# Attention and a routed mixture of experts in one kernel: gathers of tokens written ahead of gathers of weights, the token split written one group earlier, and the last tile's two blocks written to separate tiles

## The chip, the cores and the metric

The kernel runs on one core of one Trainium2 chip. The metric is device time in microseconds (us) of one execution. Three executions of the kernel before gave 2227.25, 2227.33 and 2228.41 us, median 2227.33. A further execution was recorded by the profiler; all rows quoted below come from it.

## The reference

```
def _attn_ref(u, v, z):            # u, v: 8 x 2496 x 256, z: 8 x 2496 x 64, f32
    scores = (1.0 / S) * np.matmul(z, z.transpose(0, 2, 1))
    attn = np.maximum(scores, 0.0) ** 2
    return u * np.matmul(attn, v)

def _moe_ref(x, w_gate, w1, w2):   # x: 19968 x 256, 8 experts, F = 1024
    logits = x @ w_gate
    expert_idx = np.argmax(logits, axis=1)
    ...
    gate_w = probs[np.arange(N), expert_idx]
    for e in range(E):
        mask = expert_idx == e
        xe = x[mask]
        h = np.maximum(xe @ w1[e], 0.0)
        out[mask] = gate_w[mask, None] * (h @ w2[e])
    return out
```

The attention output, reshaped to 19968 tokens of 256 values, is the input of the experts. Each token goes to one expert and is scaled by that expert's softmax probability.

## The kernel before

**Two stages.** For about the first 1310 us the attention of the 8 batches runs, and its rows are written to DRAM (`xrows`) together with the gate and the chosen expert. While it runs, lists are built that sort the tokens by expert. Then come 47 expert tiles (i = 0 to 46), and these are what the change touches. A tile holds k = 4, 3 or 2 blocks of 128 tokens of one expert. The k = 2 tiles (6, 10, 15, 17, 20, 25, 27, 31, 35, 37, 41, 46) and the k = 3 tiles (14, 24, 34, 45) are strewn among the k = 4 tiles. F = 1024 is walked in 8 slices of 128: a k = 4 or 3 tile takes one slice a step (G = 8 groups), a k = 2 tile two slices a step (G = 4 groups).

**What one tile needs.** Values are kept as a rounded part and a remainder, so that each product is three matmuls. The steps, with their lines in the profile of before:

- `load_e(i)`, L696: POOL gathers the tile's entries (token numbers and gates) into `ent`, a ring of 6. A slot comes free when the tile six earlier has had its output scattered.
- `load_x(i)`, L712: POOL gathers the tile's tokens into `rows` (ring of 3), one indirect DMA for each block. It reads the token numbers in `ent`.
- `load_w(w, h)`, L681: POOL gathers half of an expert's weights (1 MB) into a slot `s`. A slot comes free when the pieces cut from it have been read.
- `split_piece(q)`: ScalarE (ACT) L731 and L733 cast a piece of the weights to a rounded copy, VectorE (DVE) L732 and L734 subtract. The results are tiles `t` or `s`.
- `turn_x(i)`, L742: DVE transposes 32 x 32 cells of `rows` into a buffer `th`; then SP sends it to DRAM and back (L745, L747, `far`) into a second buffer `th`. The ring `th` has 3 buffers.
- `split_x(i)`: ACT L757 casts the turned tokens, DVE L758 subtracts. It frees one buffer `th`.
- `up(gi)`: PE L775 (tokens times first weights, into `ph`), ACT L779 relu, DVE L780 remainder. It is written two groups ahead of its use.
- `down(gi)`: PE L796 and L798 add into `y` (two PSUM tiles for a tile of 3 or 4 blocks, one for 2).
- `finish(i)`: ACT L806 and DVE L807 scale `y` by the gate into an output tile, POOL L809 scatters it, one indirect DMA for each block. Reading `y` frees it for the next tile.

**What sets the order.** `tiles()` writes these steps in program order, as the code printed below shows; a scheduler then orders the instructions of each engine by dependences and modelled times. What is wrapped in `pinned` goes right behind the last instructions written; `split_x` is, `turn_x` is not. On the chip each engine takes its instructions in the scheduled order. At a tile's first group (g = 0) the weights of later pieces are written first, then `load_x(i + 3)` and `load_e(i + 4)`; `turn_x(i + 2)` is written at g = G/2, and `split_x(i + 1)` at g = G - 3: group 5 of 8, or 1 of 4.

**The end.** After tile 46 (k = 2) each engine loads a count (`values_load`, L992) and branches on it: for these inputs the further tiles are skipped (L1014, L1016).

Of the kernel before, what the change touches and what calls it, by code (L numbers as in the profile page):

```python
# [8 lines left out]
F32 = mybir.dt.float32  # L9
# [10 lines left out]
P = 128  # L20
KQ = 64
G, R = 4, 32
D = 256
E = 8
F = 1024
QC = 512
# [22 lines left out]
def fused_kernel(ctx: ExitStack, tc: tile.TileContext, zt, ut, v, wg, wcat, out):  # L49
    nc = tc.nc  # L50
    B, _, SP = zt.shape
# [3 lines left out]
    NTOK = B * S  # L55
# [8 lines left out]
    BS, SS = BIG // P, SMALL // P  # L64
    ND, NB, N3, NS = split_sizes(NTOK - NA * 2 * BIG)
# [3 lines left out]
    ps2 = ctx.enter_context(tc.tile_pool(name="ps2", bufs=2, space=PSUM))  # L69
    ps1 = ctx.enter_context(tc.tile_pool(name="ps1", bufs=3, space=PSUM))  # L70
    psm = ctx.enter_context(tc.tile_pool(name="psm", bufs=1, space=PSUM))
# [9 lines left out]
    def ring_f():  # L81
        return sb.tile([P, 2, QC], F32, name="tf", tag="tf", bufs=3)
# [280 lines left out]
    def pinned(work):  # L363

        last = {}
        for i in nc.cur_bb.bb.instructions[-400:]:
            last[i.engine] = i
        with ExitStack() as behind:
            for i in last.values():
                behind.enter_context(tc.issue_after(i))  # L370
            work()
# [284 lines left out]
    MAIN = 12  # L656
# [6 lines left out]
    NM = len(order)  # L663
# [3 lines left out]
    own = [t not in seconds[which] for which, t, _ in order]  # L667
    wof = [sum(own[:i + 1]) - 1 for i in range(NT)]
# [8 lines left out]
    def load_w(w, h):  # L677
        which, t, _ = order[first_of[w]]
        wr = slot(free[0])
        free.append(free.pop(0))  # L680
        nc.gpsimd.indirect_dma_start(out=wr, out_offset=None, in_=wcat,  # L681
                                     in_offset=bass.IndirectOffsetOnAxis(ap=lists[which]["widx"][:, h, t:t + 1], axis=0))
        weights[w, h] = wr
# [100 lines left out]
    def down(gi, hh, hl):  # L784
        i, g = groups[gi]
        k = blocks[i]
        n = k * P
        w2 = pieces[piece_of[gi]][1]
        if g == 0:
            yts[i] = [ps2.tile([P, 2, QC], F32, name=f"y{s}", tag="ps2") for s in range(-(-k // 2))]  # L790
        for s in range(k):
            for c in range(fs_of[i]):
                f = g * fs_of[i] + c
                y = yts[i][s // 2][:, s % 2, :]
                cs = slice(c * n + s * P, c * n + (s + 1) * P)
                nc.tensor.matmul(y, lhsT=hh[:, cs], rhs=w2[:, f % 2].rearrange("p i d -> p (i d)"),  # L796
                                 start=f == 0, stop=False)
                nc.tensor.matmul(y[:, 0:D], lhsT=hl[:, cs], rhs=w2[:, f % 2, 0, :], start=False, stop=f == NF - 1)  # L798

    def finish(i):  # L800
        which, t, k = order[i]
        yo = ring_f().rearrange("p a (b d) -> p (a b) d", d=D)
        for s in range(k):
            y = yts[i][s // 2][:, s % 2, :]
            gate = ents[i][:, s, 0:1]
            nc.scalar.mul(yo[:, s, :], y[:, D:2 * D], gate)  # L806
            nc.vector.scalar_tensor_tensor(yo[:, s, :], y[:, 0:D], gate, yo[:, s, :], op0=ALU.mult, op1=ALU.add)  # L807
        for s in range(k):
            d = nc.gpsimd.indirect_dma_start(  # L809
                out=out, out_offset=token(i, s),  # L810
                in_=yo[:, s, :], in_offset=None, bounds_check=NTOK - 1, oob_is_err=False)
            for o in outs:
                tc.declare_no_dep(d.ins, o.ins, reason="rows are distinct")
            outs.append(d)
        del ents[i]
# [145 lines left out]
    def tiles(lo, hi, n_pieces):  # L961

        mine = [gi for gi, (i, _) in enumerate(groups) if lo <= i < hi]
        for gi in mine:
            i, g = groups[gi]
            G = NF // fs_of[i]
            if bg:
                pinned(bg.pop(0))
            if g == 0:
                for w, h in ((wof[i] + 1, 1), (wof[i] + 2, 0)):  # L970
                    if own[i] and w <= wof[hi - 1]:
                        load_w(w, h)
                if i + 3 < hi:
                    load_x(i + 3)
                if i + 4 < hi:
                    load_e(i + 4)
            ahead = min(gi + LU, mine[-1])
            while n_pieces < min(piece_of[ahead] + LP + 1, NPC * (wof[hi - 1] + 1)):
                split_piece(n_pieces)
                n_pieces += 1  # L980
            if i + 2 < hi and g == G // 2:
                turn_x(i + 2)
            if i + 1 < hi and g == G - 3:
                pinned(lambda: split_x(i + 1))
            if gi + LU <= mine[-1]:
                hs[gi + LU] = up(gi + LU)
            down(gi, *hs.pop(gi))
            if g == G - 1:
                finish(i)

    tiles(0, NM, n_pieces)
    needed = nc.values_load(lists["F"]["ns"], min_val=0, max_val=NS)  # L992

    def more(lo, hi):

# [15 lines left out]
        hs.update({gi: up(gi) for gi in range(first, first + LU)})  # L1011
        tiles(lo, hi, NPC * w + LP + 1)

    with tc.If(needed > MAIN):  # L1014
        more(NM, NM + 3)
        with tc.If(needed > MAIN + 3):  # L1016
            more(NM + 3, NT)


# [30 lines left out]
```

## Time and profile before

| | |
|---|---|
| median of 3 executions | 2227.33 us (2227.25 to 2228.41) |
| the profiled execution | 2225.69 us |
| its span | 2223.9 us |
| mean granted clock of PE | 0.997 |
| PE busy | 2197.9 us (99%) |
| DVE busy | 1678.0 us (75%) |
| ACT busy | 1313.2 us (59%) |
| POOL busy | 697.4 us (31%) |
| DMA, mean over the span | 194 GB/s |

The profiled execution is 1.64 us under the median, and its span 1.79 us under its own time; what lies around the span is outside the profile. A row of the timeline, as quoted further down, has the start in us, the duration, the engine, the line, the operation, output<-inputs, and in brackets how long the engine stood idle before it and whose end it waited for. Rows with x2 are two instructions in a row.

### The profile page before, as it was taken

The numbers are of one execution on the slowest core, as the hardware profiler recorded it, in microseconds if no ns is written. First come the engines' busy times: TensorE is split into PE (matmuls) and PEld (weight loads), VectorE is DVE, ScalarE is ACT, GpSimd is POOL, SyncE is SP. The second block draws the span as 40 slices with busy tenths as digits, with TensorE's granted clock in tenths as the row PEclk, the third lists the DMA queues.
The fourth block names the chain that finished last, engine by engine and source line by source line (L and its number), as shares of the span: only waits on it lengthen the run. The fifth ranks groups of instructions, "written<-read, shape, count | busy, mean of one in ns | idle before, by whom it ended". The sixth has DMA issues, their size and how long they took to land.

```text
span 2223.9 us, 32938 instructions
## 1 busy us (share of the span) xinstructions
PE 2197.9 (99%) x11664; PEld 1854.1 (83%) x11664; DVE 1678.0 (75%) x2782; ACT 1313.2 (59%) x1808; POOL 697.4 (31%) x720
## 2 busy tenths in 40 slices
PE   9999999999999999999999999999999999999997
PEld 6888888888888888888888888888888888888886
DVE  9888888888888888888888787566565575666653
ACT  8658657657667667667577544445454454554543
POOL 3010220220220220310222644455455455555521
PEclk9999999999999999999999999999999999999998
DMA  7966867858868758768857884565465465656530
GB/s 248 260 174 219 240 154 234 233 153 246 223 166 242 222 151 256 209 165 255 214 148 219 221 265 146 160 193 167 148 215 184 151 209 175 199 164 218 170 106 23
DMA packets 271884, 430.64 MB, mean 194 GB/s; under 512 B 109099, under 2 KB 167152, under 8 KB 252256
## 3 DMA queue, kind: packets, MB, share of 16 engines
q1 hardware_dynamic: 239200, 308.92, 48.8%
q0 software_dynamic: 32512, 119.55, 16.9%
q8 instruction: 93, 1.52, 0.3%
q14 instruction: 79, 0.65, 0.1%
HBM read 262.68 MB, written 166.20 MB: 193 GB/s over the span
## 4 chain that ended last, share of the span: by engine, by line
PE 90%; DVE 3%; DMA 2%; issue 2%; ACT 1%; POOL 1%; SPq 0%; POOLq 0%; DVEq 0%; ACTq 0%
PE ph L775 17%; PE acc L359 15%; PE acc L356 15%; PE acc L358 15%; PE y L796 12%; PE y L798 6%; PE ps_s L321 4%; PE ps_s L322 4%; PE pt L411 1%; DMA scr<-s 1%; DMA rows<-xrows,ent 1%; POOL out_dram L809 0%; POOL rows L712 0%; DVE tlo L335 0%; ACT tf L329 0%
## 5 line engine op out<-in xcount | busy, mean ns | idle before, releaser
L480 POOL DMA_INDIRECT lst<-gw,posi x160 | 201.3, 1258 | 872.0 <-DVE posi L477 535.6
L359 PE MATMUL acc<-thi,t 128*128 128x512 f32 (+1 forms) x1200 | 461.3, 386 | 0.0
L356 PE MATMUL acc<-thi,t 128*128 128x512 f32 (+1 forms) x1200 | 450.5, 386 | 0.6 <-DVE thi L333 0.6
L358 PE MATMUL acc<-tlo,t 128*128 128x512 f32 (+1 forms) x1144 | 443.0, 387 | 1.1 <-DVE tlo L335 1.1
L780 DVE SCALAR_TENSOR_TENSOR t<-ph,t 128x512 fp32r<-128x512 f32 (+1 forms) x328 | 220.0, 672 | 227.5 <-ACT t L779 223.6
L779 ACT ACTIVATE t<-ph 128x512 fp32r<-128x512 f32 (+1 forms) x328 | 192.8, 588 | 334.8 <-PE ph L775 304.2
L796 PE MATMUL y<-t,t 128*128 128x512 f32 x1062 | 378.6, 396 | 1.4 <-DVE tf L807 1.4
L775 PE MATMUL ph<-thi,t 128*128 128x512 f32 (+2 forms) x1248 | 375.6, 360 | 0.5 <-DVE t L780 0.3
L329 ACT ACTIVATE tf<-ps_s 128x1024 f32<-128x1024 f32 (+2 forms) x240 | 229.0, 962 | 184.4 <-PE ps_s L322 184.0
L798 PE MATMUL y<-t,t 128*128 128x256 f32 x1062 | 290.0, 281 | 2.6 <-DVE t L780 2.6
L356 PEld LDWEIGHTS acc<-thi,t 128*128 128x128 f32 x1200 | 225.3, 188 | 41.7 <-DVE thi L333 1.1
L359 PEld LDWEIGHTS acc<-thi,t 128*128 128x128 f32 x1200 | 225.3, 188 | 39.5
L775 PEld LDWEIGHTS ph<-thi,t 128*128 128x128 f32 x1248 | 225.5, 189 | 37.5 <-DVE t L780 1.9
L358 PEld LDWEIGHTS acc<-tlo,t 128*128 128x128 f32 x1144 | 214.9, 188 | 40.6 <-DVE tlo L335 3.4
L330 ACT ACTIVATE tf<-tf 128x1024 f32<-128x1024 f32 (+2 forms) x240 | 237.1, 998 | 5.9
L796 PEld LDWEIGHTS y<-t,t 128*128 128x128 f32 x1062 | 197.9, 188 | 43.2 <-DVE tf L807 1.9
L268 DVE STREAM_TRANSPOSE s<-tf 128x1024 f32<-128x1024 f32 x160 | 197.0, 1233 | 45.1 <-ACT tf L330 44.9
L775 PE MATMUL ph<-tlo,t 128*128 128x512 f32 (+2 forms) x624 | 224.7, 360 | 2.2 <-DVE tlo L758 2.2
L809 POOL DMA_INDIRECT out_dram<-tf,ent x160 | 166.5, 1041 | 191.6 <-DVE tf L807 151.2
L798 PEld LDWEIGHTS y<-t,t 128*128 128x128 f32 x1062 | 200.4, 189 | 13.9 <-DVE t L780 2.9
L712 POOL DMA_INDIRECT rows<-xrows,ent x160 | 164.6, 1029 | 105.1 <-DMA ent<-lst,lfeidx 60.5
L335 DVE TENSOR_TENSOR tlo<-tf,thi 128x1024 fp32r<-128x1024 f32 (+1 forms) x168 | 190.7, 1138 | 9.0 <-ACT thi L333 8.6
(237 smaller groups left out, 3929.8 us busy)
## 6 DMA issues: line engine op xcount, KB each, us to landing
scr<-s SPq DMA_DIRECT2D x80, 1024.0 KB
s<-scr SPq DMA_DIRECT2D x320, 256.0 KB
vr<-in_v_dram SPq DMA_DIRECT2D x80, 256.0 KB
u<-in_ut_dram SPq DMA_DIRECT2D x32, 512.0 KB
xrows<-th SPq DMA_DIRECT2D x128, 128.0 KB
far<-th SPq DMA_DIRECT2D x31, 512.0 KB
th<-far SPq DMA_DIRECT2D x124, 128.0 KB
lst<-pad SPq DMA_DIRECT2D x16, 624.0 KB
```

The costliest lines, as they stand in the source:

```text
L268: nc.vector.transpose(out=to, in_=a.rearrange("p i (t s k) -> p i t s k", t=4, s=G))
L329: nc.scalar.activation(a[:, :, m:n], ps[:, :, m:n], AF.Relu)
L330: nc.scalar.activation(a[:, :, m:n], a[:, :, m:n], AF.Square)
L356: nc.tensor.matmul(acc[d][:, :n], lhsT=vh, rhs=hi[:, i, :n], start=first and i == 0, stop=False)
L358: nc.tensor.matmul(acc[d][:, :n], lhsT=vh, rhs=lo[:, i, :n], start=False, stop=False)
L359: nc.tensor.matmul(acc[d][:, :n], lhsT=vl, rhs=hi[:, i, :n], start=False, stop=last and i == 1)
L480: i = nc.gpsimd.indirect_dma_start(out=lst, out_offset=bass.IndirectOffsetOnAxis(ap=posi[:m, j:j + 1], axis=0), in_=gw[:m, j, :], in_offse ...
L775: nc.tensor.matmul(o, lhsT=w1[:, part, dd, fs], rhs=xx[:, dd, :n], start=p == 0, stop=p == 5)
L779: nc.scalar.activation(hh[:, :m], ph[:, :m], AF.Relu)
L780: nc.vector.scalar_tensor_tensor(hl[:, :m], ph[:, :m], 0.0, hh[:, :m].bitcast(F32), op0=ALU.max, op1=ALU.subtract)
L796: nc.tensor.matmul(y, lhsT=hh[:, cs], rhs=w2[:, f % 2].rearrange("p i d -> p (i d)"), start=f == 0, stop=False)
L798: nc.tensor.matmul(y[:, 0:D], lhsT=hl[:, cs], rhs=w2[:, f % 2, 0, :], start=False, stop=f == NF - 1)
```

## The change

Four edits in the expert stage:

1. At a tile's first group, `load_x(i + 3)` and `load_e(i + 4)` are written ahead of the two `load_w`.
2. `split_x(i + 1)` of a tile with 8 groups is written at group 4 in place of 5. With 4 groups it stays at 1.
3. In the last tile (46) block 1 accumulates in a PSUM tile of its own (`yl`, of the pool `psm`), and each of the two blocks gets an output tile of its own.
4. `values_load` is written at the last tile's first group. In the scheduled order the load stays where it was on every engine: behind its last instruction of tile 46.

```
@@ down
+            pairs_ = [ps2.tile([P, 2, QC], F32, name=f"y{s}", tag="ps2") for s in range(-(-k // 2))]
+            yts[i] = [pairs_[s // 2][:, s % 2, :] for s in range(k)]
+            if i == NM - 1:
+                yts[i][1] = psm.tile([P, QC], F32, name="yl", tag="psm")
...
@@ finish
-        yo = ring_f().rearrange("p a (b d) -> p (a b) d", d=D)
+        yos = [ring_f().rearrange("p a (b d) -> p (a b) d", d=D) for _ in range(k if i == NM - 1 else 1)] * k
         for s in range(k):
-            y = yts[i][s // 2][:, s % 2, :]
+            yo = yos[s]
+            y = yts[i][s]
...
@@ tiles
+            if i == NM - 1 and g == 0:
+                needed.append(nc.values_load(lists["F"]["ns"], min_val=0, max_val=NS))
             if g == 0:
-                for w, h in ((wof[i] + 1, 1), (wof[i] + 2, 0)):
-                    if own[i] and w <= wof[hi - 1]:
-                        load_w(w, h)
                 if i + 3 < hi:
                     load_x(i + 3)
                 if i + 4 < hi:
                     load_e(i + 4)
+                for w, h in ((wof[i] + 1, 1), (wof[i] + 2, 0)):
+                    if own[i] and w <= wof[hi - 1]:
+                        load_w(w, h)
...
-            if i + 1 < hi and g == G - 3:
+            if i + 1 < hi and g == G // 2 + G // 8 - 1:
                 pinned(lambda: split_x(i + 1))
```

What the scheduler makes of it on DVE and POOL is shown at three places. The number behind a name tells one buffer from another.

The first place is **DVE in tile 26**, where the tokens of tile 30 are turned (`th_19393`, from their gathered `rows`), among the remainders L780 of tile 26 (`t2`, with the groups 4 to 7 in a row), the weight pieces (L732, L734) and the split of tile 27's tokens (L758). Before:

```order
L780 SCALAR_TENSOR_TENSOR t2_18978<-ph_18970,t2_18977 128x512
L734 TENSOR_TENSOR t4_19066<-s1_18907,t4_19066 128x2x256
L780 SCALAR_TENSOR_TENSOR t2_18997<-ph_18989,t2_18996 128x512
L732 TENSOR_TENSOR t4_19158<-s5_18909,t4_19158 128x512
L732 TENSOR_TENSOR s2_19096<-s1_18907,s2_19096 128x512
L734 TENSOR_TENSOR s2_19096<-s1_18907,s2_19096 128x2x256
L780 SCALAR_TENSOR_TENSOR t2_19031<-ph_19023,t2_19030 128x512
L758 TENSOR_TENSOR tlo_19043<-th_18850,thi_19042 128x512
L742 STREAM_TRANSPOSE th_19393<-rows_19151 128x4x8x32
L780 SCALAR_TENSOR_TENSOR t2_19054<-ph_19046,t2_19053 128x512
```

The same stretch of DVE after the change, where the split of tile 27 stands seven rows further up:

```order
L780 SCALAR_TENSOR_TENSOR t2_18978<-ph_18970,t2_18977 128x512
L734 TENSOR_TENSOR t4_19066<-s1_18914,t4_19066 128x2x256
L780 SCALAR_TENSOR_TENSOR t2_18997<-ph_18989,t2_18996 128x512
L732 TENSOR_TENSOR t4_19158<-s5_18916,t4_19158 128x512
L742 STREAM_TRANSPOSE th_19393<-rows_19147 128x4x8x32
L732 TENSOR_TENSOR s2_19096<-s1_18914,s2_19096 128x512
L734 TENSOR_TENSOR s2_19096<-s1_18914,s2_19096 128x2x256
L780 SCALAR_TENSOR_TENSOR t2_19035<-ph_19027,t2_19034 128x512
L780 SCALAR_TENSOR_TENSOR t2_19054<-ph_19046,t2_19053 128x512
```

The split has freed its buffer `th`, and the transpose has moved up past two weight pieces and the remainder of group 6, which now stand behind it. So do most others: the transposes of 37 tiles now stand ahead of rows that they stood behind, tile 11's ahead of the remainders of groups 5 and 6 of tile 7 and two weight pieces, tile 22's ahead of the remainders of groups 5 and 6 of tile 18, tile 42's ahead of the remainders of groups 3 to 6 of tile 38, and tile 41's ahead of two rows of the finish of tile 36.

The second place is **DVE in tile 15**, where tile 19's tokens are turned (`th_17276`), among the remainders of tile 15 (`t2`), the finish of tile 14 (`tf_16797`) and the weight pieces. Before:

```order
L780 SCALAR_TENSOR_TENSOR t2_16788<-ph_16774,t2_16787 128x512
L807 SCALAR_TENSOR_TENSOR tf_16797<-y0_16622,ent_15826,tf_16797 128x256
L807 SCALAR_TENSOR_TENSOR tf_16797<-y1_16623,ent_15826,tf_16797 128x256
L742 STREAM_TRANSPOSE th_17276<-rows_16959 128x4x8x32
L732 TENSOR_TENSOR t4_16891<-s3_16813,t4_16891 128x512
L780 SCALAR_TENSOR_TENSOR t2_16844<-ph_16830,t2_16843 128x512
L734 TENSOR_TENSOR t4_16892<-s3_16813,t4_16892 128x2x256
L807 SCALAR_TENSOR_TENSOR tf_16797<-y0_16622,ent_15826,tf_16797 128x256
L780 SCALAR_TENSOR_TENSOR t2_16880<-ph_16866,t2_16879 128x512
```

And DVE there after the change:

```order
L780 SCALAR_TENSOR_TENSOR t2_16788<-ph_16774,t2_16787 128x512
L811 SCALAR_TENSOR_TENSOR tf_16797<-y0_16622,ent_15822,tf_16797 128x256
L811 SCALAR_TENSOR_TENSOR tf_16797<-y1_16623,ent_15822,tf_16797 128x256
L732 TENSOR_TENSOR t4_16891<-s3_16820,t4_16891 128x512
L811 SCALAR_TENSOR_TENSOR tf_16797<-y0_16622,ent_15822,tf_16797 128x256
L780 SCALAR_TENSOR_TENSOR t2_16844<-ph_16830,t2_16843 128x512
L734 TENSOR_TENSOR t4_16892<-s3_16820,t4_16892 128x2x256
L742 STREAM_TRANSPOSE th_17276<-rows_16955 128x4x8x32
L780 SCALAR_TENSOR_TENSOR t2_16880<-ph_16866,t2_16879 128x512
```

Here the transpose has gone back, behind the remainder `t2_16844` (group 2 of tile 15), a weight piece and a row of the finish.

The third place is **POOL around tile 36**: entries (L696), tokens (L712: `rows_21104` are tile 40's, the next ones tile 41's), weights (L681) and scatters of tiles 35 and 36 (L809, in the other kernel L813). Before:

```order
L696 DMA ent_20869<-lst_73,lfeidx_13526 128x64
L809 DMA out_0_dram<-tf_20849,ent_19953 19968x256
L681 DMA s1_21242<-in_wcat_dram,lfwidx_13525 128x2048
L712 DMA rows_21104<-xrows_72,ent_20869 128x256 x2
L809 DMA out_0_dram<-tf_20849,ent_19953 19968x256
L712 DMA rows_21104<-xrows_72,ent_20869 128x256 x2
L696 DMA ent_21109<-lst_73,lfeidx_13526 128x32
L712 DMA rows_21246<-xrows_72,ent_21109 128x256 x2
L681 DMA s5_21244<-in_wcat_dram,lfwidx_13525 128x2048
L681 DMA s3_21657<-in_wcat_dram,lfwidx_13525 128x2048
```

POOL there after the change, where tile 40's tokens are `rows_21100` and tile 41's `rows_21242`:

```order
L696 DMA ent_20865<-lst_73,lfeidx_13526 128x64
L813 DMA out_0_dram<-tf_20849,ent_19949 19968x256
L712 DMA rows_21100<-xrows_72,ent_20865 128x256 x4
L681 DMA s1_21247<-in_wcat_dram,lfwidx_13525 128x2048
L813 DMA out_0_dram<-tf_20849,ent_19949 19968x256
L681 DMA s5_21249<-in_wcat_dram,lfwidx_13525 128x2048
L696 DMA ent_21105<-lst_73,lfeidx_13526 128x32
L712 DMA rows_21242<-xrows_72,ent_21105 128x256 x2
L681 DMA s3_21664<-in_wcat_dram,lfwidx_13525 128x2048
```

Tile 40's four gathers stand in a row ahead of the weights, but one more gather of weights (`s5_21249`) now stands ahead of tile 41's entries and tokens. In the whole stage tokens or entries change places with a gather of weights for six tiles: tokens go ahead for tiles 8, 40 and 42, and for tiles 19, 20 and 41 weights go ahead of entries or tokens. Elsewhere POOL's order of these two kinds is what it was.

More of the change, by code (lines that the diff above doesn't have):

```diff
@@ L789, in down @@
         if g == 0:
-            yts[i] = [ps2.tile([P, 2, QC], F32, name=f"y{s}", tag="ps2") for s in range(-(-k // 2))]
+            pairs_ = [ps2.tile([P, 2, QC], F32, name=f"y{s}", tag="ps2") for s in range(-(-k // 2))]
+            yts[i] = [pairs_[s // 2][:, s % 2, :] for s in range(k)]
+            if i == NM - 1:
+                yts[i][1] = psm.tile([P, QC], F32, name="yl", tag="psm")
         for s in range(k):
@@ L801, in finish @@
         which, t, k = order[i]
-        yo = ring_f().rearrange("p a (b d) -> p (a b) d", d=D)
+        yos = [ring_f().rearrange("p a (b d) -> p (a b) d", d=D) for _ in range(k if i == NM - 1 else 1)] * k
         for s in range(k):
-            y = yts[i][s // 2][:, s % 2, :]
+            yo = yos[s]
+            y = yts[i][s]
             gate = ents[i][:, s, 0:1]
@@ L810, in finish @@
                 out=out, out_offset=token(i, s),
-                in_=yo[:, s, :], in_offset=None, bounds_check=NTOK - 1, oob_is_err=False)
+                in_=yos[s][:, s, :], in_offset=None, bounds_check=NTOK - 1, oob_is_err=False)
             for o in outs:
@@ L989, in tiles @@
                 finish(i)
+    assert blocks[NM - 1] == SS
+    needed = []
     tiles(0, NM, n_pieces)
-    needed = nc.values_load(lists["F"]["ns"], min_val=0, max_val=NS)
     def more(lo, hi):
@@ L1012, in more @@
         tiles(lo, hi, NPC * w + LP + 1)
-    with tc.If(needed > MAIN):
+    with tc.If(needed[0] > MAIN):
         more(NM, NM + 3)
-        with tc.If(needed > MAIN + 3):
+        with tc.If(needed[0] > MAIN + 3):
             more(NM + 3, NT)
```

## The prediction

> **What bounds the kernel now.** I read the page first: the busy shares, then the chain that ended last.
>
> ```profile
> PE 2197.9 (99%) x11664; PEld 1854.1 (83%) x11664; DVE 1678.0 (75%) x2782; ACT 1313.2 (59%) x1808; POOL 697.4 (31%) x720
> ...
> PE 90%; DVE 3%; DMA 2%; issue 2%; ACT 1%; POOL 1%; SPq 0%; POOLq 0%; DVEq 0%; ACTq 0%
> ```
>
> PE is busy 99% of the span and is 90% of the chain, so an edit that leaves PE's matmuls as they are can only take away, or add, time in which PE stands idle. The change leaves their number and shapes alone. Next comes the view of what PE waited for, cut to the expert stage (1309 to 2224 us).
>
> ```profile
> PE y L798 <- DVE t L780: 2.6, 1, 2.6
> PE ph L775 <- DVE tlo L758: 2.2, 3, 0.7
> PE y L796 <- DVE tf L807: 1.4, 1, 1.4
> PE ph L775 <- DVE t L780: 0.3, 1, 0.3
> ```
>
> These four rows add up to 6.5 us, 0.29% of the time: that is the most that the first two edits can win, and all of it comes through DVE. Then I asked what held DVE up at its transposes of tokens (L742).
>
> ```profile
>   DMA rows<-xrows,ent: 9.1, 4
> ```
>
> Four times, 9.1 us together, DVE stood at a transpose whose gathered tokens had not landed. The two largest, in DVE's timeline:
>
> ```profile
> 1625.58 1.25 DVE L742 STREAM_TRANSPOSE th<-rows 128x1024 f32<-128x1024 f32 x1 [5.09 <-DMA rows<-xrows,ent]
> 1626.74 0.65 DVE L732 TENSOR_TENSOR t<-s,t 128x512 fp32r<-128x512 f32 x1
> 1627.32 0.68 DVE L780 SCALAR_TENSOR_TENSOR t<-ph,t 128x512 fp32r<-128x512 f32 x1
> ...
> 1836.47 1.25 DVE L742 STREAM_TRANSPOSE th<-rows 128x1024 f32<-128x1024 f32 x1 [2.11 <-DMA rows<-xrows,ent]
> ```
>
> The first (tile 19's transpose, in tile 15) held a remainder L780 behind it until 1627.32: that is PE's wait of 2.6. The second (tile 30's, in tile 26) cost PE nothing, since only the remainder of a group far ahead stood behind it. So the reader is to ask at each transpose: when do its rows land, and what stands behind it on DVE?
>
> **The change part by part.**
>
> *The transpose of tile 19 goes back.* By the order, the remainder of group 2 of tile 15 now stands ahead of it. It no longer waits, so PE's 2.6 goes: **-2.6**. What is late next is the remainder of group 3, behind the transpose. Its rows, on POOL:
>
> ```profile
> 1613.50 0.96 POOL L681 DMA_INDIRECT s<-in_wcat_dram,lfwidx  x1 [0.30 <-DVE th L742]
> 1615.37 0.95 POOL L712 DMA_INDIRECT rows<-xrows,ent  x1 [0.92 <-DMA ent<-lst,lfeidx]
> ...
> 1620.40 0.94 POOL L712 DMA_INDIRECT rows<-xrows,ent  x1 [0.30 <-issue]
> ```
>
> The transpose at 1625.58 began 5.18 after the last gather was issued; a group of a k = 2 tile gives PE about 2.8 us of work, and so the next remainder has that much more time. The weights' gather, 0.96 + 0.30 in POOL's time, now stands ahead of the entries, where POOL had been idle. I count nothing for either.
>
> *The finish of tile 34 behind tile 39's transpose* is PE's wait of 1.4:
>
> ```profile
> 1997.18 1.25 DVE L742 STREAM_TRANSPOSE th<-rows 128x1024 f32<-128x1024 f32 x1 [1.48 <-DMA rows<-xrows,ent]
> 1998.35 0.83 DVE L807 SCALAR_TENSOR_TENSOR tf<-y,ent,tf 128x256 f32<-128x256 f32 x2
> ```
>
> There the order keeps the finish behind the transpose, puts one weight piece more between them (0.6), and POOL's order of tile 39's gathers is the same. Against that, one transpose earlier the loop through DRAM runs sooner and may be out of the gathers' way. Bounds: the transpose does without its 1.48 (-1.4 + 0.6, some -0.9), or starts where it does (+0.6). I take **-0.4**, since the gathers' transfers have less beside them.
>
> The 2.2 us of L758 (three waits of at most 0.7) stay: around the splits of tiles 7 and 11 the order is the same, and the third waits for the loop through DRAM at a k = 2 tile, where the split stays at group 1.
>
> *Splits one group sooner.* Their inputs turned far ahead, so they find their data; 1.23 us of DVE move ahead of remainders that are ready well before PE asks for them. An example, the remainder of group 6 in tile 26:
>
> ```profile
> 1833.07 0.69 DVE L780 SCALAR_TENSOR_TENSOR t<-ph,t 128x512 fp32r<-128x512 f32 x1
> ...
> 1838.35 0.40 PE L775 MATMUL ph<-thi,t 128*128 128x256 f32 x2
> ```
>
> It ended at 1833.76, and by the place in its new order PE gets to it at 1838.35, 4.6 later. Cost nothing. What hides it is that lead; without it each would cost up to 1.2.
>
> *Transposes that go ahead.* A split frees the buffer that a transpose needs, and the scheduler moves 37 of them up. At five places their rows are not there yet by the times of the trace, and a wait stands ahead of remainders or a finish. The price of one place is: last gather issued, plus the time to the transpose's start, plus the transpose and what stands between, less the moment at which PE, in the new order, asks for the remainder. The shortest start after an issue is that of tile 30: its last gather was issued at 1833.47, its transpose began at 1836.47, 3.0 later; tile 19's took 5.18. I take 3.0, as four of five places have no weights in flight right ahead, and keep 5.18 for the range. A transpose passes on after 1.16, a piece takes 0.6, a remainder 0.69 to its end.
>
> ```profile
> 1833.47 0.94 POOL L712 DMA_INDIRECT rows<-xrows,ent  x1 [0.30 <-issue]
> 1837.64 0.65 DVE L780 SCALAR_TENSOR_TENSOR t<-ph,t 128x512 fp32r<-128x512 f32 x1
> ```
>
> Tile 30 (in tile 26): the rows land as before, 1836.47 + 1.16 + two pieces 1.2 + 0.69 = 1839.5 for the remainder of group 6. PE asks for it at 1838.35: **+1.2**.
>
> ```profile
> 1466.37 0.94 POOL L712 DMA_INDIRECT rows<-xrows,ent  x1 [0.30 <-issue]
> 1470.80 0.28 PE L798 MATMUL y<-t,t 128*128 128x256 f32 x1
> ...
> 1679.87 0.95 POOL L712 DMA_INDIRECT rows<-xrows,ent  x1 [0.30 <-DMA out_dram<-tf,ent]
> 1683.91 0.28 PE L798 MATMUL y<-t,t 128*128 128x256 f32 x1
> ```
>
> Tile 11 (in tile 7): 1466.37 + 3.0 + 1.16 + 0.6 + 0.69 = 1471.8 for the remainder of group 5, asked for at 1470.80: **+1.0**. Tile 22 (in tile 18): 1679.87 + 3.0 + 1.16 + 0.69 = 1684.7 against 1683.91: **+0.8**. In both POOL's gathers are held by their entries, which the change doesn't bring sooner.
>
> ```profile
> 2040.10 0.98 POOL L696 DMA_INDIRECT ent<-lst,lfeidx  x1 [3.96 <-ACT t L731]
> 2041.38 1.39 POOL L681 DMA_INDIRECT s<-in_wcat_dram,lfwidx  x1 [0.30 <-DVE tf L807]
> 2044.16 0.94 POOL L712 DMA_INDIRECT rows<-xrows,ent  x1 [1.39 <-issue]
> 2047.92 0.94 POOL L712 DMA_INDIRECT rows<-xrows,ent  x1 [0.30 <-issue]
> ...
> 2050.12 0.40 PE L796 MATMUL y<-t,t 128*128 128x512 f32 x1
> ...
> ent<-lst,lfeidx POOLq DMA_INDIRECT x45, 2.4
> ```
>
> Tile 42 (in tile 38): its four gathers now stand ahead of the weights. They wait for the entries alone, 2040.10 + 2.4 + 0.3 = 2042.8, 1.36 sooner than 2044.16; the last is issued at 2046.56. + 3.0 + 1.16 + 0.69 = 2051.4 for the remainder of group 3, asked for at 2050.12: **+1.3**. Had the gathers not moved, it would be 2.7.
>
> ```profile
> 2023.21 1.43 POOL L712 DMA_INDIRECT rows<-xrows,ent  x1 [0.30 <-issue]
> 2024.94 0.94 POOL L681 DMA_INDIRECT s<-in_wcat_dram,lfwidx  x1 [0.30 <-DVE t L732]
> ...
> 2032.80 0.62 PE L775 MATMUL ph<-thi,t 128*128 128x512 f32 x2
> ```
>
> Tile 41 (in tile 37): one gather of weights goes ahead of its entries. In the trace it was issued at 2024.94, behind tile 41's tokens; its slot comes free with a piece's subtraction shortly before. If it goes at 2023.6 to 2024.9, entries follow 1.25 later, tokens 2.7 after them, the second 1.25 later, the transpose 3.0 after that: 2031.8 to 2033.1. Now two rows of the finish of tile 36 stand behind it: 0.6 + 0.87, so 2033.3 to 2034.6, and PE asks for the accumulator they free at about 2033.0 (its place in the new order). That is 0.3 to 1.6: **+1.0**.
>
> The five make +5.3. At tiles 32, 40 and 46 the same sum leaves PE 0.4 to 0.6 us to spare, at all others over 1.5.
>
> *Weights later on POOL.* Their first reader is the cast on ACT:
>
> ```profile
> L731 ACT CAST t<-s 128x512 fp32r<-128x512 f32 x115 | 71.2, 619 | 63.8 <-PE y L798 50.9 <-PE ph L775 12.8
> ```
>
> All of its idle time but 0.1 ended with PE, none with a DMA, so a gather of weights that goes 4 or 5 places (5 to 6 us) later costs nothing while it lands ahead of its cast; if one came late, it would show here, at up to that much.
>
> *The last tile.* By PE's new order block 0 ends three matmuls ahead of block 1, about 0.47 us.
>
> ```profile
> 2210.36 0.47 ACT L806 ACTIVATE tf<-y,ent 128x256 f32<-128x256 f32 x1 [4.99 <-PE y L798]
> 2210.87 0.48 DVE L807 SCALAR_TENSOR_TENSOR tf<-y,ent,tf 128x256 f32<-128x256 f32 x1 [4.77 <-ACT tf L806]
> ...
> 2211.63 0.98 POOL L809 DMA_INDIRECT out_dram<-tf,ent  x1 [5.30 <-DVE tf L807]
> 2211.89 0.48 DVE L807 SCALAR_TENSOR_TENSOR tf<-y,ent,tf 128x256 f32<-128x256 f32 x1 [0.54 <-ACT tf L806]
> 2212.92 0.98 POOL L809 DMA_INDIRECT out_dram<-tf,ent  x1 [0.30 <-issue]
> ```
>
> The second scatter goes 1.29 after the first (0.98 + 0.30), which goes 0.76 after block 0's L807 began. So the end moves with block 0: **-0.5**, from 0 (if the first scatter must wait as before) to -0.9.
>
> Sum: -2.6 - 0.4 + 5.3 - 0.5 = **+1.8** on the profiled execution's 2225.69, which is 1.64 under the median: 2227.5, or 2229.1 as a median. I say 2229.
>
> A page weighed against it: the Trainium skill, "DMA: Bandwidth & Descriptors", section "Anatomy of one DMA — SWDGE (gpsimd) path", gives 2.0 us plus the bytes at 436 GB/s for one DMA; a token gather of 128 x 256 floats (131 KB) would take an estimated 2.3 us. The trace has 3.0 and 5.18 from issue to use with other transfers beside. By the page the five places would cost some 0.7 us less each, and the sum would be -1.7 in place of +1.8.
>
> **The rivals.**
>
> *The waits cost nothing* (rows land sooner, or the remainders have more lead than I read). Then -2.6 - 0.4 - 0.5 = -3.5: 2223.8. For it: tile 30's transpose waited 2.11 already without harm; gathers meet fewer weights. Against it: the remainders now directly behind the transposes.
>
> *DVE's waits grow* (slower). Mechanism: gathers land late, as at tile 19, 5.18 after the issue in place of 3.0. Each of the five places then costs 2.2 more, and tiles 32, 40 and 46 1.6 to 1.8 each. It decides from 3.7 us after the issue, where 0.7 more at each of the five places makes +5.3. With half of the 2.2 at all places: +1.8 + 5.5 + 1.8 = +9 (2236); with it at two or three places +4.4 to +6.6 more, 2233 to 2236. For it: the trace's 5.18 beside weights; against it: three of four recorded waits were short.
>
> *The change does little*: the scheduler's order matters less than its names suggest, the old wait of 2.6 moves to another place, only the end gains: -0.5, 2226.8.
>
> *More than that*: all waits of PE gone, -7: 2220.3. Rows and order speak against it, since two of the three kinds keep their order.
>
> **How the numbers follow.** Forecast (a sum between -1 and +4.4) 0.45, waits cost nothing 0.22, little 0.08, waits grow 0.21, more 0.04. What a measurement here can tell from no change is about 0.2%, 4.45 us: faster is under 2222.9, slower over 2231.8. Faster: the last case and a little of the second, 0.06. Slower: waits grow, and an edge of the forecast, 0.24. Same: 0.70. The range takes in the second case and most of the slower one: 2223.3 to 2235.
>
> **What would show it.** Right: PE's wait of 2.6 for L780 in tile 15 is gone; DVE stands at L742 for rows a dozen times or so, several times the 9.1 us of before, with tiles 11, 22, 30 and 42 among the longest; PE gets waits of about 1 us for L780 in tiles 7, 18, 26, 38 and for L807 in tile 37; the last matmul to the end is half a microsecond shorter. Wrong: idle time at L742 without new waits of PE (the first rival), or PE's waits over 2 us each (the second).

## The result, and the profile after

| | median | runs | ratio to before, 95% interval |
|---|---|---|---|
| before | 2227.29 us | 4 | |
| after | 2243.19 us (2240.43 to 2247.19) | 4 | 1.0072 (1.0054 to 1.0090) |

The change makes the kernel 0.7% slower, 15.9 us by the medians. The forecast was 2229, its range ended at 2235. The profiled execution of the changed kernel took 2247.19 us (span 2245.2), the slowest of the four, so its rows show 21 us where the medians show 16.

First, what PE waited for in the expert stage after the change (total, times, longest, in us):

```profile
PE y L799 <- DVE tf L811: 8.0, 3, 6.6
PE y L801 <- DVE t L780: 4.8, 4, 2.1
PE y L799 <- ACT t L779: 3.4, 1, 3.4
PE ph L775 <- DVE t L780: 2.7, 3, 0.9
PE ph L775 <- DVE tlo L758: 2.2, 3, 0.7
```

21.1 us in place of 6.5. Two single waits, 6.6 and 3.4, make up most of the growth; the rest is waits of 0.2 to 2.1 us. Next, what DVE waited for at its transposes:

```profile
  DMA rows<-xrows,ent: 72.4, 16
```

16 waits for rows in place of 4, 72.4 us in place of 9.1. Three of them in DVE's timeline (tiles 11, 30 and 41), with PE's rows that waited behind them:

```profile
1476.02 1.25 DVE L742 STREAM_TRANSPOSE th<-rows 128x1024 f32<-128x1024 f32 x1 [7.70 <-DMA rows<-xrows,ent]
...
1843.62 1.25 DVE L742 STREAM_TRANSPOSE th<-rows 128x1024 f32<-128x1024 f32 x1 [6.70 <-DMA rows<-xrows,ent]
...
2048.27 0.71 DVE L742 STREAM_TRANSPOSE th<-rows 128x512 f32<-128x512 f32 x1 [8.27 <-DMA rows<-xrows,ent]
2048.90 0.83 DVE L811 SCALAR_TENSOR_TENSOR tf<-y,ent,tf 128x256 f32<-128x256 f32 x2
```

```profile
1478.50 0.38 PE L801 MATMUL y<-t,t 128*128 128x256 f32 x1 [1.62 <-DVE t L780]
...
1637.62 0.39 PE L801 MATMUL y<-t,t 128*128 128x256 f32 x1 [0.83 <-DVE t L780]
...
1689.57 0.39 PE L801 MATMUL y<-t,t 128*128 128x256 f32 x1 [0.23 <-DVE t L780]
...
1846.69 0.45 PE L801 MATMUL y<-t,t 128*128 128x256 f32 x1 [2.07 <-DVE t L780]
...
2010.03 0.50 PE L799 MATMUL y<-t,t 128*128 128x512 f32 x1 [1.05 <-DVE tf L811]
...
2050.89 0.77 PE L799 MATMUL y<-t,t 128*128 128x512 f32 x1 [6.57 <-DVE tf L811]
```

The rows are those of the tiles 7, 15, 18, 26, 35 and 37. At tiles 7, 18 and 26 the forecast had 1.0, 0.8 and 1.2 and the rows show 1.62, 0.23 and 2.07: right in kind, and not far off in sum (3.0 and 3.9). At tile 37 it had 1.0, and the row shows 6.57. POOL's timeline says why: first after, then the same entries and tokens (tile 41's) before.

```profile
2028.26 0.95 POOL L712 DMA_INDIRECT rows<-xrows,ent  x1 [0.30 <-issue]
2029.51 0.95 POOL L681 DMA_INDIRECT s<-in_wcat_dram,lfwidx  x1 [0.30 <-issue]
2030.76 1.02 POOL L813 DMA_INDIRECT out_dram<-tf,ent  x1 [0.30 <-issue]
2033.73 1.17 POOL L681 DMA_INDIRECT s<-in_wcat_dram,lfwidx  x1 [1.94 <-DVE t L734]
2036.23 1.05 POOL L696 DMA_INDIRECT ent<-lst,lfeidx  x1 [1.33 <-DMA out_dram<-tf,ent]
2044.04 0.95 POOL L712 DMA_INDIRECT rows<-xrows,ent  x1 [6.76 <-DMA ent<-lst,lfeidx]
2045.29 0.95 POOL L712 DMA_INDIRECT rows<-xrows,ent  x1 [0.30 <-issue]
```

```profile
2019.42 0.95 POOL L696 DMA_INDIRECT ent<-lst,lfeidx  x1 [0.30 <-issue]
2021.96 0.95 POOL L712 DMA_INDIRECT rows<-xrows,ent  x1 [1.59 <-DMA ent<-lst,lfeidx]
```

Tile 41's entries take a slot of the ring that tile 35's scatter must free. That scatter (2030.76) now stands behind all four gathers of tile 40's tokens, where it stood behind two of them; it landed just ahead of 2036.23, and POOL stood 1.33 us for it. The entries themselves then go out 2.5 us behind a second gather of weights and take 7.8 us to the first use (2036.23 to 2044.04), where before they took 2.5. So DVE stands 8.27 us for the tokens, the transpose stands ahead of the finish of tile 36, that finish frees the accumulator, and PE stands.

The wait of 3.4 is at the very start of the stage. ACT after, and PE:

```profile
1315.17 1.04 ACT L757 CAST thi<-th 128x1024 fp32r<-128x1024 f32 x1 [6.78 <-DMA th<-far]
1316.12 0.59 ACT L779 ACTIVATE t<-ph 128x512 fp32r<-128x512 f32 x1
```

```profile
1316.76 0.73 PE L799 MATMUL y<-t,t 128*128 128x512 f32 x2 [3.41 <-ACT t L779]
```

Tile 1's split has moved ahead of six relus of tile 0. Its tokens were turned only late in the attention stage and were still on their way back from DRAM; ACT stood 6.78 us, the relu behind it came late, and PE stood.

The long stops cost more than themselves. The table of stretches (length, then busy time and instructions of PE, PEld, DVE, ACT and POOL, then the granted clock as a share of PE's full speed, DMA share, GB/s) around the 3.4 and the 6.6, then behind tiles 7 and 26:

```profile
1313.00:1317.00 4.00, 0.59 (x3) 0.24 (x2) 0.26 (x1) 1.83 (x3) 0.65 (x1) 1.00 0.25 70
1317.00:1322.00 5.00, 5.00 (x36) 4.13 (x36) 5.00 (x8) 0.68 (x2) 1.55 (x1) 0.66 0.42 75
```

```profile
2051.00:2055.00 4.00, 4.00 (x13) 3.42 (x14) 3.66 (x7) 2.33 (x5) 2.94 (x3) 0.50 0.64 241
2055.00:2059.00 4.00, 4.00 (x22) 3.42 (x21) 2.15 (x4) 2.07 (x4) 1.10 (x1) 0.99 0.28 89
```

```profile
1478.50:1482.30 3.80, 3.80 (x20) 3.28 (x21) 3.80 (x7) 1.22 (x2) 1.50 (x1) 1.00 0.52 182
1846.70:1850.50 3.80, 3.80 (x16) 3.51 (x17) 3.80 (x6) 0.00 (x0) 1.65 (x3) 0.55 0.77 227
```

The same of the kernel before, behind its stops of 2.6 at tile 15 and 1.4 at tile 35:

```profile
1628.20:1632.00 3.80, 3.80 (x13) 3.13 (x14) 3.80 (x8) 0.62 (x1) 0.98 (x1) 0.60 0.54 197
1999.20:2003.00 3.80, 3.77 (x21) 3.30 (x22) 3.80 (x7) 1.34 (x3) 2.52 (x3) 1.00 0.97 327
```

Behind the stops of 2.07, 3.41 and 6.57 us the mean granted clock of the next 4 to 5 us was 0.50 to 0.66. What that lost is estimated as the length times what the clock lacks: 0.50 over 4.00 us is 2.0, 0.66 over 5.00 is 1.7, 0.55 over 3.80 is 1.7; behind the 1.62 at tile 7 it stayed at 1.00. The kernel before lost 0.40 x 3.80 = 1.5 once, at tile 15. That it lost anything there is not the rule: in e1 (below), whose profile has the same stop at tile 15, 2.52 us long, the clock stayed at 1.00:

```profile
1627.70:1631.50 3.80, 3.80 (x20) 3.24 (x21) 3.80 (x7) 1.53 (x3) 0.98 (x1) 1.00 0.53 194
```

By this estimate the stops at tiles 0 and 37 cost 3.41 + 1.7 and 6.57 + 2.0 in the profiled execution, 13.7 us together. Of the span's 21.3, the waits' growth is 21.1 - 6.5 = 14.6 and the clock's 5.4 - 1.5 = 3.9, 18.5 together; 0.6 is there already before the expert stage, and some 2 us are not in these rows.

At the end the scatters go out 0.84 and 2.13 after PE's last matmul, in place of 1.30 and 2.59: the 0.46 that was forecast. From that matmul to the span's end it took 13.75 in place of 13.61, since the last scatter took longer to land.

### The profile page after: what moved, and what is told of

Read it like the earlier page. It is cut to its first block, busy times and chain, and to the rows that moved or that the text cites. A ratio compares the mean times of both kernels' runs of the same rounds, so it can differ in the third digit from the quotient of the medians.

```text
span 2245.2 us, 32887 instructions
## 1 busy us (share of the span) xinstructions
PE 2205.4 (98%) x11664; PEld 1857.3 (83%) x11664; DVE 1671.2 (74%) x2782; ACT 1311.8 (58%) x1808; POOL 698.0 (31%) x720
## 5 line engine op out<-in xcount | busy, mean ns | idle before, releaser
L480 POOL DMA_INDIRECT lst<-gw,posi x160 | 196.0, 1225 | 873.2 <-DVE posi L477 537.6
L775 PE MATMUL ph<-thi,t 128*128 128x512 f32 (+2 forms) x1248 | 377.9, 361 | 2.7 <-DVE t L780 2.7
L780 DVE SCALAR_TENSOR_TENSOR t<-ph,t 128x512 fp32r<-128x512 f32 (+1 forms) x328 | 217.9, 672 | 210.8 <-ACT t L779 208.4
L775 PEld LDWEIGHTS ph<-thi,t 128*128 128x128 f32 x1248 | 226.5, 189 | 41.5 <-DVE t L780 4.1
L775 PE MATMUL ph<-tlo,t 128*128 128x512 f32 (+2 forms) x624 | 225.3, 361 | 2.2 <-DVE tlo L758 2.2
L813 POOL DMA_INDIRECT out_dram<-tf,ent x160 | 172.2, 1076 | 172.6 <-DVE tf L811 130.9
L712 POOL DMA_INDIRECT rows<-xrows,ent x160 | 166.2, 1039 | 125.2 <-DMA ent<-lst,lfeidx 77.4
```

Source lines behind the costliest of these rows:

```text
L480: i = nc.gpsimd.indirect_dma_start(out=lst, out_offset=bass.IndirectOffsetOnAxis(ap=posi[:m, j:j + 1], axis=0), in_=gw[:m, j, :], in_offse ...
L775: nc.tensor.matmul(o, lhsT=w1[:, part, dd, fs], rhs=xx[:, dd, :n], start=p == 0, stop=p == 5)
L780: nc.vector.scalar_tensor_tensor(hl[:, :m], ph[:, :m], 0.0, hh[:, :m].bitcast(F32), op0=ALU.max, op1=ALU.subtract)
```

## The experiments

The kernels ran in four sets, each with the kernel before on the same chip. Its median was 2225.74 us in the first set, and 2234.19, 2233.63 and 2232.39 in the others, so ratios are compared, not times. A ratio is not the quotient of the two medians; the two differ by up to 0.0012. Where three runs share a row, the interval of each ratio reaches 0.0012 to 0.0016 to either side.

| run | what | median | ratio to before, 95% interval |
|---|---|---|---|
| e1 | change, split back | 2227.66 | 1.0006 (0.9997 to 1.0015) |
| e2 | before, split alone | 2244.53 | 1.0088 (1.0074 to 1.0101) |
| e3 | change, first split back | 2241.59 | 1.0076 (1.0062 to 1.0090) |
| e4 | change, transposes held | 2234.00 | 1.0039 (1.0025 to 1.0052) |
| e5, e10, e14 | e3 with 8 entry buffers | 2240.80, 2242.89, 2239.27 | 1.0031, 1.0043, 1.0040 |
| e6, e11, e15 | before with 8 entry buffers | 2241.93, 2241.55, 2237.59 | 1.0037, 1.0025, 1.0029 |
| e7, e12, e16 | before, transposes held | 2224.10, 2223.59, 2220.74 | 0.9964, 0.9952, 0.9960 |
| e8 | e3 with transposes held | 2227.32 | 0.9968 (0.9957 to 0.9979) |
| e9 | the change again | 2251.42 | 1.0068 (1.0050 to 1.0086) |
| e13 | the kernel before as control | 2231.98 | 1.0004 (0.9989 to 1.0018) |

**Which edit.** e1 undoes the split, e2 makes it alone:

```diff
-            if i + 1 < hi and g == G // 2 + G // 8 - 1:   # e1, in the change
+            if i + 1 < hi and g == G - 3:
```

```diff
-            if i + 1 < hi and g == G - 3:                 # e2, in the kernel before
+            if i + 1 < hi and g == G // 2 + G // 8 - 1:
```

Expected of e1:

> The changed kernel with the token split of the tiles of 8 groups back at group 5; gathers of tokens first and the last tile's two blocks apart stay. Theory S (the split alone does the harm; in the scheduled order the written place of the loads moves nothing in the 47 tiles that run): 2226.5 to 2228.0, as before, with PE's waits of 2.6 at tile 15 and 1.4 at tile 35 back. Rival L (the loads' order does it): 2240 to 2246. Of the last tile alone: from PE's end to the span's end 13.57 before, 13.71 after; if its edit wins the 0.5 of the forecast, this kernel shows some 13.1.

Expected of e2:

> The kernel before with one line changed: the split of tiles of 8 groups at group 4. Theory S: 2240 to 2247, as the whole change. Rival L: 2226 to 2229.

e1 is the kernel before again (1.0006), with PE's 2.5 at tile 15 and 1.4 at tile 35 in its profile; e2 is the whole change (1.0088). The split alone does it. In the scheduled order the loads' written place moves nothing in the 47 tiles: POOL's instructions of the stage stand in e1's trace in the order of before and in e2's in that of the change, so what looks on POOL like a change of the loads follows from the split, too. Of the last tile, e1 took 13.20 from PE's end to the span's end and e2, without that edit, 13.61; the nine profiles with it lie at 13.04 to 13.85 (mean 13.35), the nine without it at 13.49 to 13.66 (mean 13.59). The scatters are 0.46 sooner in each; the landing of the last one varies by more than that.

**The first stop.** e3 splits tile 1 where it was split before:

```diff
-            if i + 1 < hi and g == G // 2 + G // 8 - 1:
+            if i + 1 < hi and g == (G - 3 if i == 0 else G // 2 + G // 8 - 1):
```

> The changed kernel, with the split of tile 1 alone (written in tile 0) back at group 5. After the change ACT stands 6.78 us at tile 1's cast until its tokens are back from DRAM, PE waits 3.4 for the relu behind it, and the granted clock in that stretch is 0.92; tile 0 takes 27.4 us in place of 22.25. Theory S1 (this first wait costs its gap and a slower clock behind it): 5 us less than the changed kernel, 2236 to 2241, and tile 0 again at 22.3. Rival (the gap alone, the clock is chance): 3.6 less. Rival (the wait only moves to the next use of those tokens): no less, 2240 to 2246.

The stretch 1309 to 1345 in e2, with the early first split, and in e3:

```profile
1309.00:1345.00 36.00, 32.54 (x170) 26.56 (x169) 25.47 (x88) 11.25 (x21) 15.52 (x15) 0.91 0.49 143
```

```profile
1309.00:1345.00 36.00, 36.00 (x205) 30.05 (x204) 31.05 (x112) 13.88 (x26) 15.41 (x15) 1.00 0.51 148
```

PE is busy throughout and the clock stays at 1.00: the stop and the slow clock behind it go together. The time does not show what they cost. Against e2 the median is 2.9 us lower (the profiled spans by 7.3, 2242.7 and 2235.4), where 5 was expected; but the intervals overlap, and by its ratio, 1.0076, e3 is no faster than the change itself (1.0072, and 1.0068 in e9). The executions of e3 lie up to 8 us apart.

**Transposes held.** e4 writes each transpose at the start of the tile two ahead of its own, and pins it there:

```diff
-            if i + 2 < hi and g == G // 2:
-                turn_x(i + 2)
+            if i + 2 < hi and g == (1 if G == 8 else 0):
+                pinned(lambda: turn_x(i + 2))
```

> The changed kernel, with the transposes of tokens held in their written place: pinned, at group 1 of a tile of 8 groups and group 0 of one of 4, so that they come one to two tiles later and find their rows. Theory T (the transposes that moved ahead of their rows hold DVE, and with it PE): all waits of DVE for rows go, the wait of 6.6 at tile 37 and those of 1 to 2 at tiles 7, 26 and 41 go, and so does the old 2.6 of tile 15; what stays is tile 0's stall of 5: 2228 to 2233. Rival D (the splits themselves, or the DMA traffic, hold PE): 2240 or more. Rival late (turned tokens now come late for their split): new waits at L757, 2233 to 2245.

What PE waited for in e4:

```profile
PE ph L775 <- ACT thi L757: 5.7, 1, 5.7
PE y L799 <- ACT t L779: 3.4, 1, 3.4
PE ph L775 <- DVE tlo L758: 2.2, 3, 0.7
PE ph L775 <- DVE t L780: 1.6, 1, 1.6
PE y L799 <- DVE tf L811: 1.0, 3, 0.4
```

No wait of DVE for rows is left, and with them went the 6.6 at tile 37 and the waits behind remainders at tiles 7, 15, 18 and 26. The 3.4 at tile 0 stays, as expected. What was not expected is the 5.7: at tiles 3 and 4 the pinned transposes stand behind the building of the lists, and tile 3's split came late. The time, 2234.00, is 1 us over theory T's range. So theory T holds for these waits, and the rival "late" has its place, too. e8 and e7 leave the first tiles alone (tile 6 is the first one held, and at group 0), e8 in the change with the first split back, e7 in the kernel before:

```diff
-            if i + 2 < hi and g == G // 2:
-                turn_x(i + 2)
+            if i + 2 < hi and g == (0 if 4 <= i < NM else G // 2):
+                pinned(lambda: turn_x(i + 2)) if 4 <= i < NM else turn_x(i + 2)
```

Expected of e7:

> The kernel before, with each transpose from tile 6 on held at the first group of the tile two ahead of its own, pinned. Turned tokens lay 25 to 56 us unused before, so this should delay no split. All waits of DVE for rows go, with PE's 2.6 and 1.4: 4 us under the kernel before. If the loop through DRAM (6 to 17 us) is late at a tile of two blocks, PE shows a wait for a split (L757, L758) of 1 to 6 us there and the gain is gone.

Expected of e8:

> The changed kernel with the first split back at group 5 and the transposes from tile 6 on held as in the run before. If the earlier split is worth anything by itself once the transposes stay, it is under that run; my theory says it is not (its inputs and its lead were there already): both within 1.5 us of each other, 3 to 5 us under the kernel before. If the split itself holds the engines, it is 2 us or more over it.

e7 is 0.36% under the kernel before and e8 0.32%. Early or late, no difference of the split is shown once the transposes stay: the ratios are 0.9 us apart and their intervals overlap, while the medians, 3.2 us apart in favour of the late split, miss the 1.5 that was expected. Nothing is gained by the early split itself.

**Late rows.** e5 keeps the early transposes and gives the entries two buffers more; e6 does that alone in the kernel before:

```diff
-        en = ents[i] = sb.tile([P, BS, ENT], F32, name="ent", bufs=6)
+        en = ents[i] = sb.tile([P, BS, ENT], F32, name="ent", bufs=8)
```

Expected of e5:

> The changed kernel with the first split back (as in the run before) and 8 buffers in place of 6 for the entries. The transposes keep their early places on DVE, but entries and tokens no longer wait for the scatter of the tile six before, so they are gathered a tile or more sooner. Theory R (the early transposes cost only because their rows land late, and the rows are late because their entries wait behind scatters and weights): the waits of DVE for rows, 69.8 us in 16, fall to under 10; PE's 6.3 at tile 37 and the 1 to 2 at tiles 7, 18, 26 go; what is left is under 6 us of PE's waits, so 0 to 6 us under the kernel before. Rival O (the order on DVE alone does it, whenever rows land): as the run with the first split back, 10 to 17 us over the kernel before. Rival Q (more gathers at once only queue longer in the DMA engines): between, 4 to 10 over.

Expected of e6:

> The kernel before with 8 buffers for the entries and nothing else: DVE keeps its order of transposes, remainders and finishes. By theory R PE's waits of 2.6 at tile 15 and 1.4 at tile 35 go, and with them 4 us: 2221 to 2223.5 where the kernel before gives 2226, a little faster. By rival O or Q: no change, within 1 us.

DVE's waits at transposes in e5:

```profile
  DMA far<-th: 1.7, 1
  DMA rows<-xrows,ent: 1.2, 1
```

69.8 us of waits for rows fell to 1.2, and PE's waits at tiles 26 and 37 are gone, though no transpose stands later than in e3 (ten stand earlier still). Tile 41's entries went out at 2001.21, 26 us sooner than in e3, and its tokens were gathered 37 us ahead of their transpose. So the rows were late because their entries were; that part of theory R stands. The run doesn't tell the wait for the slot from the slow landing behind weights: with this lead neither matters. Yet e5 is 0.31% over the kernel before, and e6 0.37%, where theory R had both under it. Both lost time at tile 4: there ACT stood with nothing that the profile shows as cause, and between 1380 and 1410 us PE stood 6.6 and 8.1 us, at a mean granted clock of 0.83 and 0.77. Two more sets were to tell whether the chip or the ring makes that. Expected of e9, e10, e11 and e12 (the change, e5, e6 and e7 again):

> The changed kernel itself, unchanged, beside the next three on the same chip: in the runs before these, ACT, DVE and PE stood some 100 us in sum with nothing that the profile shows as cause, which the records of the kernels before them do not have, and the kernel before took 2234 in place of 2226. Expected 13 to 20 over the kernel before, with PE's waits of 3.4 at tile 0 and 5 to 7 at tile 37.

> The changed kernel with the first split back and 8 buffers for the entries, once more. Its waits of DVE for rows had fallen from 69.8 to 1.2, and none of PE's waits of over 2 at tiles 26 and 37 was left; it lost its time where ACT stood without cause. Theory R, without such stalls: 0 to 6 under the kernel before, 10 or more under the changed kernel. Rival O: 10 or more over the kernel before.

> The kernel before with 8 buffers for the entries, once more. Theory R: PE's 2.6 at tile 15 and 1.4 at tile 35 gone, 2 to 5 under the kernel before. Rival Q (gathers that run further ahead press on the rest): 5 or more over it, with waits of PE at tiles 4 to 7 that are not without cause this time.

> The kernel before with the transposes from tile 6 on held at the first group of the tile two ahead, once more: no wait of DVE for rows, PE's 2.6 and 1.4 gone, 3 to 5 under the kernel before. If its lead over the kernel before (8 on the last chip) came from that chip's stalls alone, 0 to 2 under it.

They ran on the chip of the second set and gave the same picture: the change 0.68% over, the rings of 8 over, the held transposes 0.48% under. The last set ran on a third chip, with the kernel before as control; e14, e15 and e16 are e5, e6 and e7 once more:

> The kernel before itself, for its profile on this chip. If the chip makes the stands without cause: ACT has 40 to 100 us of them in the expert stage here too, and PE a gap of 5 us or more near tile 4 (1385 to 1405 us). If the ring of 8 makes them: none near tile 4, PE's waits 2.6 at tile 15 and 1.4 at tile 35 as in its first profile.

> The changed kernel with the first split back and 8 buffers for the entries. If the stand at tile 4 comes with the ring: PE's gaps there are 5 to 10 us again, on any chip, and it is 5 to 12 over the control. If with the chip: on another chip than in the last two sets it is 0 to 6 under the control.

> The kernel before with 8 buffers for the entries. As the run above: with the ring 5 to 10 over the control with a gap at tile 4; with the chip 2 to 5 under it, without PE's 2.6 and 1.4.

> The kernel before with the transposes from tile 6 on held at the first group of the tile two ahead: 3 to 5 under the control on a chip without stands, 8 to 10 under it on one with them.

ACT near tile 4 in e15, with the ring of 8, then in the control e13 (`remote` means that the profile does not name whose end was waited for):

```profile
1391.09 0.62 ACT L733 CAST t<-s 128x512 fp32r<-128x512 f32 x1 [9.83 <-remote]
1395.37 0.60 ACT L779 ACTIVATE t<-ph 128x512 fp32r<-128x512 f32 x1 [3.66 <-remote]
```

```profile
1386.65 0.62 ACT L733 CAST t<-s 128x512 fp32r<-128x512 f32 x1 [5.49 <-PE ph L775]
1389.57 0.60 ACT L779 ACTIVATE t<-ph 128x512 fp32r<-128x512 f32 x1 [2.30 <-PE ph L775]
```

And the stretch 1380 to 1410 in the same two:

```profile
1380.00:1410.00 30.00, 22.16 (x88) 16.54 (x87) 10.05 (x15) 7.01 (x12) 17.24 (x18) 0.77 0.42 131
```

```profile
1380.00:1410.00 30.00, 29.86 (x154) 25.03 (x153) 16.17 (x25) 12.11 (x22) 18.37 (x19) 1.00 0.58 196
```

With the ring of 8, ACT stood 9.83 us where the control stood 5.49, PE then stood 8 us, and its mean granted clock was 0.77. The control has no such stop, nor has e16, so on this chip it comes with the ring. It is large enough for the 6 to 9 us by which e14 and e15 are over the control; whether it is all of them was not tried. What ACT waited for there is not in the records, and whether the ring would win on the first set's chip, where no such stands were recorded, was not tried.

**A kernel that beats both.** e16's PE waits:

```profile
PE ph L775 <- issue: 1.5, 2, 0.7
PE ph L775 <- DVE tlo L758: 0.7, 1, 0.7
PE y L798 <- DVE t L780: 0.3, 1, 0.3
PE ph L775 <- ACT thi L757: 0.2, 1, 0.2
```

Its ratio is 0.9960 (0.9947 to 0.9973), as in the two sets before (0.9964, 0.9952): 2220.74 us where the control gave 2231.98. The kernel before with its transposes later, not earlier, has hardly a wait of PE left. All three sets with held transposes ran on chips on which the kernel before takes 2232 to 2234; what holding them gains where it takes 2226, as in the first set, was not tried. Their medians, 2220.74 to 2224.10, lie 1.6 to 5.0 us under the 2225.74 of that set.

## Why the prediction was wrong, point by point

The sum forecast +1.8 us, and the medians moved by +15.9. Two steps failed: at tile 41 the term "tokens 2.7 after them", which came to 7.8, and the price of nothing for the splits, which tile 1's split did not keep. A third cost, the slower clock behind long stops, was in no term.

- *Bounds* (PE bound, 6.5 us to be won at most, all through DVE's waits for rows): right as a reading of PE's waits. The profiled spans of the control and of e16, where hardly a wait is left, differ by 7.3 (2225.4 and 2218.1); by their ratios the held transposes win 8 to 11 us, more than these waits.
- *"Splits one group sooner ... they find their data. Cost nothing."* This step failed, for one tile. It was argued from one remainder in the middle of the stage. From tile 3 on it holds: in the trace of before the turned tokens lie 25 to 56 us before their split. Tile 1's had 6.7: its loop through DRAM runs across the end of the attention stage, and ACT stood 6.78 us for it. It cost 3.41 of standing and, with the clock, an estimated 5; e3's trace shows both go, its time doesn't show their worth.
- *"Tile 41: +1.0"*: the place and the mechanism (weights ahead of its entries, the finish of tile 36 behind the transpose) were right, the size wrong: 6.57, and 8.6 with the clock. PE came to the accumulator at 2044.3, 11.3 later than the 2033.0 of the working. With these 11.3 added, the working has the entries go out between 2036.2 and 2037.5, and they went at 2036.23: the 1.33 that POOL stood for the slot did not make them later than counted. What failed is the next term, entries to tokens: 7.81 in place of 2.7, 5.1 more, which is nearly all of the 5.6 that the wait has too much. The last steps held, 1.25 between the two gathers and 2.98 from the last to the transpose. The 2.7 was taken from a median row over all entries; the trace of before has rows that stand as tile 41's now do. There tile 25's entries went out 2.2 us behind weights and took 6.2:

```profile
1722.14 0.98 POOL L681 DMA_INDIRECT s<-in_wcat_dram,lfwidx  x1 [0.30 <-issue]
1724.31 0.96 POOL L696 DMA_INDIRECT ent<-lst,lfeidx  x1 [1.20 <-DMA out_dram<-tf,ent]
1730.50 0.95 POOL L712 DMA_INDIRECT rows<-xrows,ent  x1 [5.22 <-DMA ent<-lst,lfeidx]
```

With 6.2 for the 2.7, the working would have had +4.5 in place of +1.0. e4 and e5 take the stop away from either side: by the order on DVE, or by entries that go out sooner.

- *Tiles 11, 22, 30*: forecast +1.0, +0.8 and +1.2, measured 1.62, 0.23 and 2.07. Right as waits (3.0 and 3.9 in sum); the last one cost 1.7 more by the clock.
- *Tile 42: +1.3*: DVE stood 2.9 us for its rows, but no wait of PE followed: after the stop of 6.57 and the slow clock PE itself came that much later, and the remainder was there. Terms that lie one behind the other are not a plain sum.
- *Tile 15: -2.6*: 0.83 of the wait stayed, as the next remainder stood behind the transpose, where I had counted nothing; the 1.5 of clock behind the old stop went as well, which was not counted either. In sum 3.3 in these two profiles, near the forecast; against e1, where the clock stayed at 1.00 behind this stop, it is 1.7. *Tile 35: -0.4*: 1.4 went to 1.05. Right.
- *"At all others over 1.5 to spare"*: not at the k = 3 tiles. The transposes of tiles 28 and 38 found their rows, but their own 1.2 us now stands ahead of a remainder; that is the growth of PE's waits at L775 behind L780 from 0.3 to 2.7, with tile 45's transpose, which waited 2.2 for its rows, as the third.
- *The last tile: -0.5*: the scatters are 0.46 sooner, in every profile with that edit; in the time it is lost in the spread of the last landing.
- *The clock* was in no term. Every wait was priced at its length; by the estimate those of 2.07, 3.41 and 6.57 cost 1.7 to 2.0 more each in the profiled execution, and the 2.6 that went had cost 1.5, which e1's 2.52 did not.
- *The rival "waits grow"* was on the right side, but with the wrong mechanism: the transposes of tiles 11, 22 and 30 began within 0.9 us of the moment that was counted, once the time by which PE came later there is added. From the last gather to the transpose it took 2.76 to 2.98 us at all five places, the 3.0 that the forecast took and not the rival's 5.18. Two long stops make most of the difference in the profile, and the forecast had one of them at 0 and the other at a seventh.

## What to carry to other kernels

A move by one group frees a buffer, and a scheduler that fills freed buffers at once moves what waits for them, too: read in the new order what now stands ahead of which waiting instruction on each in-order engine, and follow each wait back through its whole chain (slot, scatter, entries, tokens) and not to its last link alone. Price a transfer by a row that stands in the same place, here right behind weights, and not by the median of all. Where data lie ready for 25 us, work belongs later and not sooner: here the gain was in holding the transposes back. Look at the border between two stages by itself, since leads read in the middle of a stage do not hold there, and with a stop of the bounding engine of some us look at the clock that follows it.

## What the runs showed of the hardware

- In the profiles of before and of the change, after PE had stood 2.07, 2.6, 3.4 and 6.6 us, its granted clock was 0.50 to 0.66 over the next 4 to 5 us; after stops of 1.4 and 1.62 it stayed at 1.00. The Trainium skill, "TensorE: Matmul & The Clock Gate", section "Part 1: The HAM clock gate (the "warmup" mystery)", has half rate until some 3.4 us of sustained work; 0.66 over 5 us agrees with that (3.4 us at half).
- The length alone doesn't decide for stops between 2 and 2.6 us. The clock fell behind those of 2.07 (the change), 2.20 and 2.41 (e9) and 2.60 (before), and stayed at 1.00 behind those of 2.12 (e13), 2.32 (e12) and 2.52 (e1). Behind each of the ten stops of 3.4 to 6.6 us in these profiles it fell. What decides in between is open.
- Tile 41's entries (128 x 32 floats, 16 KB), issued 2.5 us behind a gather of 1 MB of weights, took 7.8 us to their use; before, 8.1 us behind one, 2.5. In e3 it was 7.8 again, 2.7 us behind the weights. In the trace of before (from tile 6 on), seven gathers of entries went out 1.2 to 5.3 us behind weights, and it took 4.6 to 10.5 us until the first gather of their tokens; for the 34 others the median was 2.7.
- The same kernel had medians of 2226 to 2227 us on some chips and 2232 to 2234 on others; on the latter ACT and DVE stand for tens of microseconds in sum with nothing that the profile shows as cause. The kernels with held transposes have such stands, too (e16: 53 us of ACT and 56 of DVE; the control: 45 and 38). In all six runs with a ring of 8 entries PE stood 5.5 to 8.7 us between 1380 and 1410 us, at a mean clock of 0.77 to 0.83; in the six with a ring of 6 on the same two chips it stood 0.1 to 2.6, at 1.00. What makes these stands is open.
